# Turning 28 leftover dK^T/dV^T slabs in the input-gradient stage instead of the wq/wo-gradient stage

## The chip, the cores and the metric

One Trainium2 chip; the kernel runs on 1 of its cores. The metric is device time in microseconds of one execution of the whole program. Beside the timed runs there is one profiled execution, from which all rows of the profile come.

## The reference

The reference is a forward pass and its whole backward pass (a VJP). The forward normalizes `x`, runs attention over a K/V cache and a gated feed-forward layer on the same normalized input, and multiplies the two:

```python
def _fwd_reference(A_x, A_k_cache, A_v_cache, A_wq, A_wo, B_x, B_w_gate, B_w_up, B_w_down):
    def _A_ref(x, k_cache, v_cache, wq, wo):
        q = (x @ wq).reshape(B, Sq, H, Dh).transpose(0, 2, 1, 3)
        scores = jnp.einsum("bhqd,bhkd->bhqk", q, k_cache) * (Dh ** -0.5)
        p = _softmax(scores, axis=-1)
        o = jnp.einsum("bhqk,bhkd->bhqd", p, v_cache)
        return o.transpose(0, 2, 1, 3).reshape(B, Sq, H * Dh) @ wo
    def _B_ref(x, w_gate, w_up, w_down):
        h = _sigmoid(x @ w_gate) * (x @ w_up)
        return h @ w_down
    xn = _layernorm(A_x, axis=-1)
    s = _A_ref(xn, A_k_cache, A_v_cache, A_wq, A_wo)
    g = _silu(_B_ref(xn, B_w_gate, B_w_up, B_w_down))
    return A_x + s * g
```

The outputs are the forward result and the gradients of `x`, `k_cache`, `v_cache`, `wq`, `wo`, `w_gate`, `w_up` and `w_down` for a given `grad_out`. Sizes: S = 2048 positions, D = 576, H = 32 heads of Dh = 128, F = 4608; all tensors bfloat16. The gradients of the two caches have 32 x 2048 x 128 elements each, 0.52 MB a head.

## The kernel before

The kernel runs in stages, one after the other, each with its own tile pools.

1. Normalization and the first half of the feed-forward layer.
2. Its second half.
3. Attention, forward and backward, head by head. It produces dK and dV of each head **transposed**, as a slab of 128 x 2048, and puts the 64 slabs into a scratch tensor in DRAM, `kvT_d[h, k]` (k = 1 for dV, 0 for dK).
4. The output of the attention block, and the forward result.
5. The feed-forward weight gradients: a loop over 18 blocks `fb` of 256 columns of F.
6. The gradients of `wq` and `wo`: 8 groups `hg` of 4 heads. For each head two accumulations (`accumulate`, L982) of 16 row tiles with 2 matmuls each (512 and 64 columns): one gives the rows of dwo, the other the transposed dwq. ACT copies the result out of PSUM (L40). The dwo rows are stored from POOL's queue (L1143, two `dwo` buffers); dwq is turned by a transposing DMA on SP's queue (L1145) and stored per group (L990, L992). At the start of a group POOL issues the loads of the next group's attention output and dq, `onb` and `dqb` (L1010, L1013), 2 MB each. On SP, ten transposed weight pieces for the next stage (`load_T_rows`, L63) are spread over the first 20 heads. PSUM has room for four accumulations.
7. The input gradient: 8 blocks of 256 rows (`sbi`, class `Rows`), each the sum of three products with the transposed weights: du (36 row tiles of F), dg (36) and dq (32). The work is cut into 80 chunks, `seq`: 3 chunks of 12 tiles for du, 3 for dg, 4 chunks of 8 tiles for dq per block. The first two blocks run interleaved by product, so that block 0 ends at chunk 15 and block 1 at chunk 19; the others end at 29, 39 and so on to 79. A chunk is loaded by one transposing DMA on SP (`load_chunk`, L1122) into one of four buffers (two in the old `ah` tile, two called `cf`); chunk n therefore waits until TensorE is done with chunk n - 4. The matmuls are those of L1188. When a block is complete, ACT and DVE work on its two row tiles (`finish`, L1204 to L1217), and POOL stores them (`dx`, L1218); `got` loads (L1177) are issued on POOL where a block begins.

The slabs are turned to the natural layout by the pair `kv_turn` and `kv_store`: `kv_turn` takes the next slab, lets SP issue a transposing DMA from `kvT_d` into one of two `kvn` buffers (L1022), and `kv_store` lets POOL store that buffer into the output (L1028). Stage 5 calls the pair twice per block, which is 36 slabs. The 28 that are left are turned one per head in stage 6: `kv_turn` at the start of a head, `kv_store` at its end.

Two things set the order. Stages 4 to 7 run under a manual schedule for SP and POOL: each of these two queues issues its DMAs in the order in which the program text calls them, and a DMA that waits (for its data, or for a buffer) holds everything behind it on its queue. The other engines also work in program order. And a pool of a later stage takes the space of an earlier one, tile by tile as this comes free.

Of the kernel before, what the change touches and what calls it, by code (L numbers as in the profile page):

```python
# [66 lines left out]
def kernel(  # L67
# [8 lines left out]
    _, S, D = A_x.shape  # L76
    _, H, Sk, Dh = A_k_cache.shape
# [490 lines left out]
    for dead, flat in enumerate([t_[:].rearrange("p a b -> p (a b)") for t_ in (dsT, Kns[H % 2], Vn, dOn)] + [xnT_flat]):  # L568
        h0 = sum(n for _, _, n, _ in wo_parts)
        n = min(flat.shape[1] // D, H - h0)  # L570
# [314 lines left out]
    with late("pc") as pc, late("pcw") as pcw, late("pcf") as pcf, \  # L885
# [129 lines left out]
        kv_left = [(h, k) for h in range(H) for k in (1, 0)]  # L1015
        kv_wait = []

        def kv_turn(pool):
            if kv_left:
                h, k = kv_left.pop(0)  # L1020
                t_ = pool.tile([P, NT, P], bf, name="kvn", bufs=2)
                nc.sync.dma_start_transpose(t_[:], kvT_d[h, k])  # L1022
                kv_wait.append((t_, (out_2, out_3)[k][0, h]))

        def kv_store():
            if kv_wait:
                t_, dst = kv_wait.pop(0)
                nc.gpsimd.dma_start(dst.rearrange("(p t) d -> p t d", t=NT), t_[:])  # L1028
# [75 lines left out]
        seq = []  # L1104
# [14 lines left out]
        def load_chunk(n):  # L1119
            sbi, (src_d, nK, KC), k0 = seq[n]  # L1120
            v = bufs4[n % len(bufs4)][:, :KC * SB2].rearrange("p (k s) -> p k s", s=SB2)
            nc.sync.dma_start_transpose(v, src_d[sbi * SB2:(sbi + 1) * SB2, k0 * P:(k0 + KC) * P])  # L1122
            return v

        chunks = {}
        with late("c2w") as wp, late("c2b") as blk, late("c2s", 2) as sb, late("c2ps", 4, space=PSUM) as ps:
            dqTs = padded(wp, 2, "dqT")
            onqs = [(onb0, dqb0), tuple(blk.tile([P, NT, HG * P], bf, name=nm)[:] for nm in ("onb", "dqb"))]
            gap = max(1, (H - HG) // len(wT_pieces))
            for hg in range(NHG):  # L1130
                cols = slice(hg * HG * P, (hg + 1) * HG * P)
                onb, dqb = onqs[hg % 2]
                if hg + 1 < NHG:
                    load_on(onqs[(hg + 1) % 2][0], hg + 1)
                    load_dq(onqs[(hg + 1) % 2][1], hg + 1)
                dwq = dwqs[hg % 2]
                for hl in range(HG):
                    h = hg * HG + hl
                    lcols = slice(hl * P, (hl + 1) * P)
                    kv_turn(blk)  # L1140
                    dwo = sb.tile([P, D], bf, name="dwo")
                    accumulate(ps, onb, ds_all, lcols, dwo, "acc")
                    nc.gpsimd.dma_start(out_5[h * P:(h + 1) * P, :], dwo[:])  # L1143
                    accumulate(ps, dqb, xn_all, lcols, dqTs[h % 2], "acc")
                    nc.sync.dma_start_transpose(dwq[:, :, lcols], dqTs[h % 2][:])  # L1145
                    kv_store()
                    if h % gap == gap - 1 and wT_pieces:
                        load_T_rows(nc, *wT_pieces.pop(0))
                    if hg == NHG - 1 and hl < len(cf_pre) and NHG % 2 == 0:
                        chunks[hl] = load_chunk(hl)  # L1150
                store_T(out_4, cols, dwq)
            while wT_pieces:
                load_T_rows(nc, *wT_pieces.pop(0))
            while kv_left or kv_wait:
                kv_turn(blk)
                kv_store()

        with late("c4s", 2) as sb, late("c4cf") as chp, late("c4ps", 2, space=PSUM) as ps:
            wqT_sb = wd_flat[:, :H * D].rearrange("p (h d) -> p h d", d=D)
            assert H * D <= DT * F  # L1160
            wq_pieces = list(dts)
            total_k = FT * 2 + H
            cf_more = [chp.tile([P, cf_n], bf, name=f"cf{k}")[:] for k in range(2)]
            npre = len(chunks)
            order4 = list(range(len(cf_pre)))
            bufs4[:] = cf_pre + cf_more
            ahead = [npre]

            class Rows:

                def __init__(self, sbi):
                    self.sbi = sbi
                    self.accs = [[ps.tile([P, 512], f32, name=f"acc{sl}_{j}") for j in range(len(ncs))] for sl in range(nsl)]
                    self.gots = []
                    for sl in range(nsl):
                        got = sb.tile([P, D], bf, name=f"got{sl}")
                        nc.gpsimd.dma_start(got[:], go2[(sbi * nsl + sl) * P:(sbi * nsl + sl + 1) * P, :])  # L1177
                        self.gots.append(got)
                    self.k = 0

                def mul(self, ch, wT, k0, KC):
                    last = self.k + KC == total_k
                    order = [(kk, sl) for kk in range(KC) for sl in range(nsl)]
                    if last:
                        order.sort(key=lambda o: o[1])
                    for kk, sl in order:
                        for j, (n0, nn) in enumerate(ncs):
                            nc.tensor.matmul(self.accs[sl][j][:, :nn], lhsT=ch[:, kk, sl * P:(sl + 1) * P], rhs=wT[:, k0 + kk, n0:n0 + nn],  # L1188
                                             start=(self.k + kk == 0), stop=(self.k + kk == total_k - 1))
                    self.k += KC  # L1190
                    if last:
                        self.finish()

                def finish(self):
                    nj = len(ncs)
                    for sl in range(nsl):
                        st = self.sbi * nsl + sl
                        rows = slice(st * P, (st + 1) * P)
                        dxn = sb.tile([P, D], f32, name="dxn")
                        ca = sb.tile([P, nj], f32, name="ca")  # L1200
                        cb = sb.tile([P, nj], f32, name="cb")
                        junk = sb.tile([P, D], f32, name="junk")
                        for j, (n0, nn) in enumerate(ncs):
                            nc.scalar.activation(dxn[:, n0:n0 + nn], self.accs[sl][j][:, :nn], AF.Copy, accum_out=ca[:, j:j + 1])  # L1204
                            nc.vector.scalar_tensor_tensor(junk[:, n0:n0 + nn], self.accs[sl][j][:, :nn], 1.0, xn_all[:, st, n0:n0 + nn],  # L1205
                                                           op0=ALU.mult, op1=ALU.mult, accum_out=cb[:, j:j + 1])
                        cs = sb.tile([P, 2], f32, name="cs")
                        nc.vector.tensor_reduce(cs[:, 1:2], cb[:], axis=AX.X, op=ALU.add)
                        nc.vector.tensor_reduce(cs[:, 0:1], ca[:], axis=AX.X, op=ALU.add)
                        m12 = sb.tile([P, 2], f32, name="m12")  # L1210
                        nc.vector.tensor_scalar(m12[:], cs[:], -1.0 / D, None, op0=ALU.mult)
                        t = sb.tile([P, D], f32, name="t")
                        nc.vector.scalar_tensor_tensor(t[:], xn_all[:, st, :], m12[:, 1:2], dxn[:], op0=ALU.mult, op1=ALU.add)
                        t2 = sb.tile([P, D], f32, name="t2")
                        nc.vector.tensor_scalar(t2[:], t[:], m12[:, 0:1], rstd_all[:, st:st + 1], op0=ALU.add, op1=ALU.mult)
                        dx = sb.tile([P, D], bf, name="dx")
                        nc.vector.tensor_tensor(dx[:], t2[:], self.gots[sl][:], op=ALU.add)  # L1217
                        nc.gpsimd.dma_start(o1[rows, :], dx[:])  # L1218

            row_of = {}  # L1220
            for n, (sbi, which, k0) in enumerate(seq):
                if n not in chunks:
                    chunks[n] = load_chunk(n)
                if n % 2 and n >= 3 and wq_pieces:
                    load_T_rows(nc, wqT_sb, A_wq, *wq_pieces.pop(0))
                if sbi not in row_of:
                    row_of[sbi] = Rows(sbi)
                wT = wuT_sb if which is fu else wgT_sb if which is fg else wqT_sb
                if which is fq:
                    while wq_pieces:  # L1230
                        load_T_rows(nc, wqT_sb, A_wq, *wq_pieces.pop(0))
                row_of[sbi].mul(chunks.pop(n), wT, k0, which[2])
        pc3.release()


# [28 lines left out]
```

## Time and profile before

| what | value |
| --- | --- |
| five runs, us | 5067.85, 5022.1, 5056.59, 5067.54, 5031.59 |
| median of these, us | 5056.59 |
| the profiled execution, us | 5059.62 |
| its span, us | 5057.8 |
| mean granted TensorE clock | 0.988 |
| busy: TensorE, VectorE, ScalarE, GpSimd | 4896.9, 2530.7, 2501.3, 887.8 us |
| stage 6, first to last matmul, us from the span's start | 4302.2 to 4629.8 |
| stage 7, first to last matmul | 4629.8 to 5045.9 |

In the profile's rows PE is TensorE, DVE VectorE, ACT ScalarE, POOL GpSimd, SP the sync engine. A row of a group gives line, engine, output and inputs; a row of a wait reads "who, its line, <- the engine and line waited for: total us, times, longest us". A DMA is counted from its issue to its landing. The DMA share is the mean busy time of the core's 16 DMA engines; where transfers overlap in an engine it can pass 1.

### The profile page before, as it was taken

How to read it: one execution, taken by the hardware profiler on the slowest of the kernel's cores; microseconds unless marked ns; L12 is line 12 of the kernel's file. 1: busy time of each engine (PE TensorE's matmuls, PEld its weight loads, DVE VectorE, ACT ScalarE, POOL GpSimd, SP SyncE). 2: the span in 40 equal slices, each digit the busy share in tenths (PEclk: the TensorE clock that was granted, in tenths of full speed). 3: DMA queues.
4: the chain of work that ended last, by engine and by line, in shares of the span. 5: the costliest groups of instructions: out<-in, count | busy, mean ns of one | idle time of the engine just before them, and what ended most of it. 6: DMA issues, size and time to landing. Idle time of an engine off the chain costs nothing.

```text
span 5057.8 us, 102037 instructions
## 1 busy us (share of the span) xinstructions
PE 4896.9 (97%) x41029; PEld 2901.3 (57%) x41029; DVE 2530.7 (50%) x6625; ACT 2501.3 (49%) x4576; POOL 887.8 (18%) x1379
## 2 busy tenths in 40 slices
PE   9999999999999999999999999998999999878999
PEld 4445666666666666666666666665565555434554
DVE  4544665665665665665665665665254443000111
ACT  4422766666666666666666666665132222111000
POOL 3322111111111111111111111111222322111000
PEclk9999999999999999999999999999999999999999
DMA  7887999999999999999999999999899999999976
GB/s 259 273 205 171 229 231 216 231 228 226 230 231 224 225 225 228 231 223 223 235 231 222 227 235 222 227 225 230 208 223 256 235 230 261 272 256 241 172 140 120
DMA packets 3053831, 1134.86 MB, mean 224 GB/s; under 512 B 2948321, under 2 KB 2952546, under 8 KB 3053346
## 3 DMA queue, kind: packets, MB, share of 16 engines
q1 hardware_dynamic: 2944738, 771.06, 83.2%
q0 software_dynamic: 108000, 356.60, 22.6%
q8 instruction: 322, 5.28, 0.4%
q14 instruction: 163, 1.34, 0.1%
q10 hardware_dynamic: 608, 0.59, 0.0%
HBM read 175.31 MB, written 215.68 MB: 77 GB/s over the span
## 4 chain that ended last, share of the span: by engine, by line
PE 85%; DMA 8%; SPq 3%; issue 2%; DVE 2%; POOL 1%; ACT 0%; POOLq 0%; ACTq 0%; DVEq 0%
PE acc L685 18%; PE acc L746 16%; PE sp L638 9%; PE dp L708 8%; PE acc L982 8%; PE acc L1188 7%; PE acc L217 5%; PE u_ps L452 3%; PE g_ps L450 3%; PE acc L535 2%; PE dh L1059 2%; PE acc L952 2%; DMA ah<-h_d 2%; SPq L1022 1%; PE acct L147 1%
## 5 line engine op out<-in xcount | busy, mean ns | idle before, releaser
L656 ACT ACTIVATE Pq<-sp 128x1024 bf16<-128x1024 f32 x1024 | 1047.0, 1023 | 274.2 <-PE sp L638 264.9
L711 DVE SCALAR_TENSOR_TENSOR Pq<-dp,negdelta,Pq 128x1024 bf16<-128x1024 f32 x512 | 654.8, 1279 | 44.8 <-PE dp L708 44.7
L714 ACT ACTIVATE t<-dp,negdelta 128x1024 bf16<-128x1024 f32 x512 | 567.1, 1114 | 215.1 <-PE dp L708 200.5
L708 PE MATMUL dp<-VT,dOT 128*128 128x512 bf16 x2048 | 609.7, 379 | 2.2
L638 PE MATMUL sp<-KQ 128*128 128x512 bf16 x2048 | 609.5, 379 | 2.2 <-ACT Pq L656 2.1
L685 PEld LDWEIGHTS <-dST 128*128 128x128 bf16 x8192 | 508.4, 98 | 157.2 <-DMA dST<-Pq 17.2
L685 PEld LDWEIGHTS <-PT 128*128 128x128 bf16 x8192 | 500.4, 98 | 139.2 <-DMA PT<-Pq 20.2
L685 PE MATMUL acc<-Kn,dST 128*128 128x128 bf16 x8192 | 557.7, 219 | 11.4 <-DMA dST<-Pq 11.4
L685 PE MATMUL acc<-Vn,PT 128*128 128x128 bf16 x8192 | 543.0, 219 | 13.5 <-DMA PT<-Pq 13.0
L746 PE MATMUL acc<-Pq,dOn 128*128 128x512 bf16 x2048 | 531.9, 379 | 0.0
L746 PE MATMUL acc<-Pq,Qn 128*128 128x512 bf16 x2048 | 526.5, 380 | 0.0
L715 DVE TENSOR_TENSOR Pq<-t,Pq 128x1024 bf16<-128x1024 bf16 x512 | 354.4, 692 | 322.5 <-ACT t L714 308.1
L1205 DVE SCALAR_TENSOR_TENSOR junk<-acc,xn_all 128x512 f32<-128x512 f32 (+1 forms) x32 | 13.9, 453 | 718.8 <-ACT dxn L1204 718.8
L726 ACT ACTIVATE dq_n<-acc,rsc 128x128 bf16<-128x128 f32 x512 | 187.5, 366 | 339.3 <-PE acc L685 317.8
L746 PEld LDWEIGHTS <-Qn 128*128 128x128 bf16 x2048 | 200.5, 98 | 241.3 <-issue 2.4
L746 PEld LDWEIGHTS <-dOn 128*128 128x128 bf16 x2048 | 199.0, 98 | 234.5 <-issue 1.1
L638 PEld LDWEIGHTS <-KQ 128*128 128x128 bf16 x2048 | 179.2, 98 | 124.1 <-issue 3.6
L708 PEld LDWEIGHTS <-dOT 128*128 128x128 bf16 x2048 | 178.7, 98 | 124.0 <-issue 11.7
L679 POOL DMA_DIRECT2D on_d<-o_n x128 | 97.1, 759 | 782.7 <-DVE junk L697 462.2
L643 DVE TENSOR_REDUCE rs_all<-rsp 128x1 f32<-128x2 f32 x512 | 78.4, 153 | 306.3 <-ACT Pq L656 295.5
L679 POOL DMA_DIRECT2D dq_d<-dq_n x128 | 98.0, 765 | 713.0 <-ACT dq_n L726 671.4
L1060 DVE SCALAR_TENSOR_TENSOR nbl<-ah 128x256 bf16<-128x256 bf16 x288 | 98.7, 417 | 236.8 <-DMA ah<-h_d 227.6
(210 smaller groups left out, 6734.8 us busy)
## 6 DMA issues: line engine op xcount, KB each, us to landing
out_dram<-kvn POOLq DMA_DIRECT2D x64, 512.0 KB, 8.8
ah<-a_d POOLq DMA_DIRECT2D x18, 1024.0 KB, 9.6
ah<-h_d POOLq DMA_DIRECT2D x18, 1024.0 KB, 12.4
du_d<-du_blk POOLq DMA_DIRECT2D x18, 1024.0 KB, 14.5
dg_d<-dg_blk POOLq DMA_DIRECT2D x18, 1024.0 KB, 16.3
h_d<-h_row POOLq DMA_DIRECT2D x64, 256.0 KB, 3.5
a_d<-a_row POOLq DMA_DIRECT2D x64, 256.0 KB, 3.8
x_all<-in_A_k_cache_dram SPq DMA_DIRECT2D x64, 256.0 KB, 3.7
```

The source lines that it names most:

```text
L217: nc.tensor.matmul(av[:, :CH], lhsT=w[:, i, :], rhs=srcT[:, i, cs], start=(i == 0), stop=(i == DT - 1))
L638: nc.tensor.matmul(sp[:, c * CH:(c + 1) * CH], lhsT=hs.QT[:, qt * P:(qt + 1) * P], rhs=hs.KT[:, hf * HW_ + c * CH: hf * HW_ + (c + 1) * CH ...
L656: nc.scalar.activation(Pq[:, hsl], sp[:], AF.Exp, scale=SCALE, accum_out=hs.rsp[:, hf:hf + 1])
L679: nc.gpsimd.dma_start(dst_d[q0 * P:(qt + 1) * P, hs.h * P:(hs.h + 1) * P].rearrange("(t p) d -> p t d", p=P), buf[:])
L685: nc.tensor.matmul(hs.acc[:, 0, :], lhsT=T[:, kt, :], rhs=rhs[:, kt, :], start=(kt == 0), stop=(kt == NT - 1))
L708: nc.tensor.matmul(dp[:, c * CH:(c + 1) * CH], lhsT=hs.dOT[:, qt * P:(qt + 1) * P], rhs=hs.VT[:, hf * HW_ + c * CH: hf * HW_ + (c + 1) * C ...
L711: nc.vector.scalar_tensor_tensor(Pq[:, hsl], dp[:], hs.negdelta[:, qt:qt + 1], Pq[:, hsl], op0=ALU.add, op1=ALU.mult)
L714: nc.scalar.activation(t[:], dp[:], AF.Identity, bias=hs.negdelta[:, qt:qt + 1], scale=1.0)
L715: nc.vector.tensor_tensor(Pq[:, hsl], t[:], Pq[:, hsl], op=ALU.mult)
L746: nc.tensor.matmul(self.acc, lhsT=self.nat[:, qt, :], rhs=self.slabs[qt][:, cs], start=(qt == self.lo), stop=(qt == self.hi - 1))
L982: nc.tensor.matmul(accs[j][:, :nn], lhsT=lhs[:, st, cols], rhs=rhs[:, st, n0:n0 + nn], start=(st == 0), stop=(st == NT - 1))
L1188: nc.tensor.matmul(self.accs[sl][j][:, :nn], lhsT=ch[:, kk, sl * P:(sl + 1) * P], rhs=wT[:, k0 + kk, n0:n0 + nn], start=(self.k + kk == 0) ...
```

## The change

The calls of `kv_turn` and `kv_store` in the loop over heads of stage 6 are taken out, and the loop that emptied the list at its end. Stage 7 calls them instead: from chunk 10 on, at every even chunk, after the chunk's load and before its matmuls, `kv_store` of the slab before and then `kv_turn` of the next one, as many as the pace formula gives. After the last slab is turned, `kv_store` follows the matmuls of the chunk. The two `kvn` buffers now come from the pool `c4cf` of stage 7.

```diff
@@ stage 6, the loop over the heads of a group
                     lcols = slice(hl * P, (hl + 1) * P)
-                    kv_turn(blk)
                     dwo = sb.tile([P, D], bf, name="dwo")
                     accumulate(ps, onb, ds_all, lcols, dwo, "acc")
                     nc.gpsimd.dma_start(out_5[h * P:(h + 1) * P, :], dwo[:])
                     accumulate(ps, dqb, xn_all, lcols, dqTs[h % 2], "acc")
                     nc.sync.dma_start_transpose(dwq[:, :, lcols], dqTs[h % 2][:])
-                    kv_store()
...
             while wT_pieces:
                 load_T_rows(nc, *wT_pieces.pop(0))
-            while kv_left or kv_wait:
-                kv_turn(blk)
-                kv_store()
@@ stage 7, the loop over the chunks
                 if n not in chunks:
                     chunks[n] = load_chunk(n)
+                if n >= len(seq) // 8 and n % 2 == 0:
+                    for _ in range(-(-len(kv_left) // max(1, (len(seq) * 7 // 8 - n) // 2))):
+                        kv_store()
+                        kv_turn(chp)
                 if n % 2 and n >= 3 and wq_pieces:
                     load_T_rows(nc, wqT_sb, A_wq, *wq_pieces.pop(0))
...
                 row_of[sbi].mul(chunks.pop(n), wT, k0, which[2])
+                if not kv_left:
+                    kv_store()
+            while kv_left or kv_wait:
+                kv_turn(chp)
+                kv_store()
```

## The prediction

> **What bounds the kernel now.** I read four things in this order: the slices of the page, the busy times of the two last stages, the waits inside the first of them, and the queues inside the second. All durations come from the one profiled execution (5059.6 us in all, span 5057.8). It lies 3 us above the median of the five runs, 5056.6; those reach from 5022 to 5068, so that about 1% is what a measurement of this kernel can tell from no change.
>
> The slices first; 40 of 126 us each.
>
> ```profile
> PE   9999999999999999999999999998999999878999
> ```
>
> TensorE is the bound nearly everywhere. The one dip at the end is slices 34 to 36, and the stages there are the wq/wo gradients (PE from 4302.2 to 4629.8 us) and the start of the input gradient (4629.8 to the end). The next view is busy time by stretch: PE, weight loads, DVE, ACT, POOL, granted clock, DMA share, GB/s.
>
> ```profile
> 4302.00:4598.00 296.00, 231.45 (x1792) 117.14 (x1793) 0.00 (x0) 36.07 (x105) 54.59 (x83) 0.90 1.09 271
> 4598.00:4630.00 32.00, 31.60 (x259) 16.38 (x259) 0.00 (x0) 7.21 (x23) 6.15 (x11) 1.00 0.98 217
> 4660.00:4700.00 40.00, 40.00 (x328) 20.56 (x327) 0.00 (x0) 0.00 (x0) 0.00 (x0) 1.00 1.10 226
> 4760.00:5000.00 240.00, 240.00 (x1961) 124.34 (x1960) 32.17 (x100) 8.92 (x40) 9.18 (x17) 1.00 0.77 145
> ```
>
> In heads 0 to 27 of wq/wo, the heads with a slab turn, PE is busy 231 of 296 us while the DMA engines are full (1.09). In heads 28 to 31, which have none, PE is full. The input gradient keeps PE full; its DMA share is 1.10 at the start and 0.77 later. Now the waits inside wq/wo.
>
> ```profile
> POOL out_dram L1028 <- DMA kvn<-kvT_d: 246.7, 27, 18.7
> ACT dwo L40 <- DMA out_dram<-dwo: 222.6, 27, 23.9
> PE acc L982 <- ACT dwo L40: 62.2, 7, 17.5
> ```
>
> Read from the bottom: PE waits for a free accumulator, which ACT has not copied out, because the dwo buffer's store (L1143) has not landed. That store sits on POOL behind a kvn store (L1028), and POOL stands still until the slab's turn has landed. All the long PE waits stand at the start of a group of four heads, where 4 MB of the next on/dq blocks is loaded as well.
>
> **The change part by part.** 36 of the 64 slabs are turned under the feed-forward gradients, before and after. The other 28 leave the heads: 28 transposes on SP (L1022) and 28 stores on POOL (L1028), each of 0.52 MB. They reappear in the input gradient, one pair at every even chunk n from 10 to 64 of 80 (the pace formula gives 1 each time), and the last store is issued well ahead of the end, so that the last row's tail (last matmul 5045.9, span 5057.8) stays.
>
> *Taken out of wq/wo.* 64 accumulations of 3.92 us start to start (32 matmuls) are 250.9 us. The stage took 4629.8 - 4302.2 = 327.5. What is left, 76.6, is 64.8 of waits at accumulator copies (62.2 and 2.6), some 9 us of five slow restarts (5.79 instead of 4.08 us for 32 matmuls after a wait of 17.5, and the like after each of 7.7 or more; none after 3.0), one more such restart at the stage's start (1.8), and crumbs. With the slab turns gone the DMA engines carry 87.1 - 29.4 = 57.7 MB here; at the 266 GB/s of this stage 217 us, under 251. So DMA is no longer the bound, and nothing stands ahead of a dwo store but its group's loads. These still hold it for some 17 us, against two heads (15.7 us) until its buffer is wanted and two more of accumulator buffers. Best: 252.7 us, a gain of 75 (only the first restart remains). Worst: each of six group starts keeps the shortest of the long waits, 7.7 us, a gain of 29. I take 70, near the best, because heads 28 to 31 (31.5 us) and the first eight heads ran without a wait.
>
> ```profile
> 4598.40 31.52 PE acc L982 x256
> ```
>
> This is the last group in the chain that ended last: 256 matmuls, 123 ns each.
>
> *Added to the input gradient, by throughput.* Chunks 10 to 64 are 31 of 5.88 us (du/dg, 0.786 MB) and 24 of 3.92 us (dq, 0.524 MB): 276.4 us of PE. Their transposes are 37.0 MB, one late wq piece 1.05, the 28 slabs 14.7: 52.7 MB. At the 226 GB/s of the stretch 4660 to 4700, which moved almost nothing but transposes at a full share, 233 us. Plain transfers are 14.7 MB of slab stores and 3.5 of got and dx. The rate of these I work out from wq/wo, where both kinds ran at a full share:
>
> ```profile
> q1 hardware_dynamic: 128978, 32.42, 60.4%
> q0 software_dynamic: 14691, 54.38, 47.3%
> ```
>
> 32.4 MB of transposes at 226 GB/s leave 184.5 of the 328 us for 54.4 MB: 295 GB/s. So 18.2 MB are 62 us, and the sum 295 against 276: 18 us too much. If the two kinds overlap better than here, nothing; if the DMA engines also stand idle at the six row finishes described below, up to 60: SP is held for 6.4 + 5.0 us there, and the stores and got loads of that time (1.1 MB at 295 GB/s) fill 4, which leaves some 7 idle each time.
>
> The Trainium skill's page Advanced Engine Details and Errata, section X-Bar Transpose (TRN2), says that transposing transfers are as fast as plain ones and to expect 350 to 400 GB/s. The row of 226 GB/s at a share of 1.10 doesn't agree, and the measurement decides; by the page the 52.7 MB would be an estimated 151 us, this term would vanish, and the sum would be 18 us lower.
>
> *Added to the input gradient, by order.* This is the wait that takes the place of the old one. A chunk load (L1122) waits until PE is done with the chunk four before it. A slab turn waits on SP for the store of the slab two before it (two kvn buffers), and this store stands on POOL in program order, behind the dx stores (L1218) of a row that finishes at chunk f. Rows finish at f = 15, 19, 29, 39, 49 and 59 in the range of the slabs. Then the store at f+1 can't be issued before the row is finished, the turn at f+3 waits for it, and load f+4, queued behind this turn, is late; PE waits for that load. The pieces of one finish as it is now (PE, POOL and SP of the timeline):
>
> ```profile
> 4783.06 8.00 PE L1188 MATMUL acc<-wdT_sb,ah 128*128 128x512 bf16 x64
> 4791.10 2.92 SPq L1122 DMA_TRANSPOSE ah<-dg_d  x1
> 4796.95 0.55 POOL L1218 DMA_DIRECT2D out_dram<-dx  x1 [2.25 <-DVE dx L1217]
> ```
>
> PE ends chunk 29 at 4791.06; load 33 starts 0.04 us later; the second dx store is done on POOL at 6.4. After the change load 33 comes behind: 6.4, the slab store's landing 5.0 (median in wq/wo), the turn on SP 3.5 (median), and lands 5.2 later: 20.1 after the finish. PE has three chunks until then: 17.6 us where they are du/dg (five finishes, 2.5 late each), 11.8 where they are dq (f = 15, 8.3 late, and a slow restart of 1.8). Sum 22.6, taken as 23. With the shortest rows (2.9, 1.6, 4.4) it is 15.3: 3.5 late once and nothing else. With long ones (8.8, the page's median of all slab stores; 3.6; 10.3, the longest chunk landing) it is 29.1: 11.5 five times and 17.3, and six slow restarts, 86 in all.
>
> *At nothing.* POOL's 28 issues of 0.54 us and SP's issues between chunk loads (per two du/dg chunks 2 x 3.1 + 3.5 of 11.8 us): SP has the room except around n = 10, where it is one or two chunks ahead only, and that is in the throughput term. The kvn tiles' new place: the third and fourth chunk buffers wait for the last group's operands anyway (PE 6.0 us late at 4653.6); a place that frees earlier or later moves that by at most these 6 us either way.
>
> **Sum.** -70 + 18 + 23 = -29: 5059.6 - 29 = 5030.6, and 5028 from the median. I say 5030.
>
> **The rivals.** (a) *The turns hide nearly whole.* The later rows' share of 0.77 speaks for it, and that a late load is absorbed by the three loaded chunks; against it that slabs and chunks together ask for more than the transposes' rate shown. -70 + 4 + 6 for an uneven start: 5000. (b) *The order on POOL costs more than it saves; slower than before.* Place: load f+4 at six finishes. Price by the long rows 86, with the throughput term 18 and half of the lost gaps (21) 125: 5059.6 - 70 + 125 = 5115. It decides from (70 - 18)/6 = 8.7 us lost per finish; a saturated queue, where a slab took up to 31 us to land, speaks for it, and that only the slab store and one turn are in flight at that moment speaks against. (c) *The waits in wq/wo aren't the slabs' doing.* All long waits stand at group starts, with the on/dq loads; if these hold the dwo stores alone, the gain is 29, and with 41 given back the time is 5072. Against it speak the first two groups, which load as much and have no wait.
>
> **How the numbers follow.** Forecast 0.50, its own range 5008 to 5050; (a) 0.23; (b) 0.13; (c) 0.14. Below 5006 lie (a) and a little of the forecast: 0.25. Above 5107 lies rather more than half of (b): 0.09. The rest is within 1%: 0.66. The range takes in the best of (a), 4988, and leaves out most of (b) only: 4988 to 5085.
>
> **What would show it.** In the profile after: wq/wo stage of 253 to 262 us with POOL's wait at L1028 and ACT's wait at dwo nearly gone, PE full in it; the input gradient some 41 us longer; waits of PE at L1188 for cf or ah tiles right after chunks 18, 22, 32, 42, 52 and 62, of 2 to 10 us, with SP waiting at L1022 for the kvn store and POOL at L1218 ahead of it; DMA share near 1.1 from 4615 to 4900 us. If PE still waits at group starts in wq/wo, the first term is wrong; if the waits at L1188 lie anywhere else or the stage grows by more than 70 us, the second.

## The result and the profile after

The changed kernel takes 5018.0 us in the median, the kernel before 5056.6: a ratio of 0.9926, 95% interval [0.9907, 0.9945], which is 28 to 47 us less. The profiled execution has a span of 5002.9 us, 54.9 below the one before. In what follows a stage's length runs from its first matmul to the next stage's first one, the last stage's to the end of its last matmul.

| | before | after | difference |
| --- | --- | --- | --- |
| stages 1 to 5, start to first matmul of stage 6 | 4302.2 | 4293.4 | -8.8 |
| stage 6 (wq/wo) | 327.5 | 252.6 | -74.9 |
| stage 7 (input gradient) | 416.1 | 443.8 | +27.7 |
| last matmul to the end of the span | 11.9 | 13.1 | +1.2 |

The first row isn't the edit's: over the executions shown below the start of stage 6 lies between 4279 and 4337 us, whatever is changed behind it. That scatter is nearly as wide as the spread of the runs before, and is why stage lengths are used here beside the times. Where no second execution is named, a stage length is that of one profiled execution.

The start of stage 7 scatters too, with no slab in it yet. These rows of PE show the wait in its first six chunks before the change and the row with which chunk 6 begins (L1188 before the change is L1183 after it):

```profile
4653.57 8.13 PE L1188 MATMUL acc<-wuT_sb,cf 128*128 128x512 bf16 x48 [6.02 <-DMA cf<-du_d]
4673.30 11.93 PE L1188 MATMUL acc<-wgT_sb,cf 128*128 128x512 bf16 x96
```

and after:

```profile
4583.41 11.94 PE L1183 MATMUL acc<-wgT_sb,cf 128*128 128x512 bf16 x96 [0.83 <-DMA cf<-dg_d]
```

So the first six chunks took 43.6 us before and 37.5 after. The first slab is turned only behind the load of chunk 10, and the same changed kernel took 42.9 us for them in a second execution; over all executions shown here it is 35.3 to 44.9, with slabs in the stage or without. From chunk 6 to the end the stage took 372.6 us before and 406.4 after (406.8 in the second execution). The slabs' price in stage 7 is therefore better read as 33.8 us than as 27.7: the profiled execution happened to save 6.1 at the start.

The slices of the page: the dip has moved out of slices 34 to 36, and small ones have come at the end.

```profile
PE   9999999999999999999999999999899999999898
```

Busy time by stretch (PE, weight loads, DVE, ACT, POOL, clock, DMA share, GB/s), for stage 6, for the part of stage 7 with the slabs, and for what follows it:

```profile
4293.40:4546.00 252.60, 252.60 (x2049) 130.33 (x2050) 0.00 (x0) 43.44 (x126) 45.97 (x66) 0.99 0.82 228
4610.00:4915.00 305.00, 278.49 (x2218) 140.85 (x2216) 39.22 (x120) 10.72 (x48) 26.94 (x50) 0.98 1.14 227
4915.00:4990.00 75.00, 74.76 (x612) 38.30 (x608) 7.88 (x28) 2.86 (x13) 2.16 (x4) 1.00 0.71 132
```

Stage 6 has no idle PE any more, and its DMA share has fallen from 1.09 to 0.82. Stage 7 has a full DMA share while slabs are turned, and PE idles there for 26 of 305 us. The waits of stage 6, that had 222.6 us at this line:

```profile
ACT dwo L40 <- DMA out_dram<-dwo: 42.3, 5, 8.9
```

Now PE in stage 7, six of its rows that begin with a wait (the bracket gives the idle time before the row and what ended it). They are the ones at the places that the prediction named; ten more waits, of 0.5 to 2.4 us, lie elsewhere behind the start of chunk 6:

```profile
4662.40 6.06 PE L1183 MATMUL acc<-wdT_sb,cf 128*128 128x512 bf16 x32 [6.22 <-DMA cf<-dq_d]
4686.96 6.05 PE L1183 MATMUL acc<-wgT_sb,cf 128*128 128x512 bf16 x48 [0.86 <-DMA cf<-dg_d]
4741.41 6.05 PE L1183 MATMUL acc<-wgT_sb,ah 128*128 128x512 bf16 x48 [1.31 <-DMA ah<-dg_d]
4796.59 6.05 PE L1183 MATMUL acc<-wgT_sb,cf 128*128 128x512 bf16 x48 [1.25 <-DMA cf<-dg_d]
4852.15 6.05 PE L1183 MATMUL acc<-wgT_sb,ah 128*128 128x512 bf16 x48 [1.67 <-DMA ah<-dg_d]
4905.31 6.05 PE L1183 MATMUL acc<-wgT_sb,cf 128*128 128x512 bf16 x48 [0.84 <-DMA cf<-dg_d]
```

These are chunks 19, 23, 33, 43, 53 and 63, the ones the prediction named. The first also shows the slow restart (6.06 us for 32 matmuls; 4.09 where the wait was short). How the first comes about, from the rows of PE, POOL and SP:

```profile
4644.25 2.80 SPq L1122 DMA_TRANSPOSE cf<-dq_d  x1
4650.59 0.55 POOL L1213 DMA_DIRECT2D out_dram<-dx  x1 [2.32 <-DVE dx L1212]
4651.13 1.07 POOL L1028 DMA_DIRECT2D out_dram<-kvn  x2
4654.08 3.19 SPq L1022 DMA_TRANSPOSE kvn<-kvT_d  x1
4657.35 1.92 SPq L1122 DMA_TRANSPOSE cf<-dq_d  x1
```

SP stands from 4647.05 (4644.25 + 2.80) to 4654.08, since the slab's buffer is freed by a store that POOL issues only behind the dx store; the chunk load behind it starts at 4657.35, and PE waits for it until 4662.40.

### The profile page after: what moved, and what is told of

The parts are those of the page before. It is cut to its first block, busy times and chain, and to the rows that moved or that the text cites. A ratio compares the mean times of both kernels' runs of the same rounds, so it can differ in the third digit from the quotient of the medians.

```text
span 5002.9 us, 102058 instructions
## 1 busy us (share of the span) xinstructions
PE 4892.3 (98%) x41029; PEld 2897.0 (58%) x41029; DVE 2531.1 (51%) x6625; ACT 2503.9 (50%) x4576; POOL 891.1 (18%) x1379
## 4 chain that ended last, share of the span: by engine, by line
PE 87%; DMA 6%; issue 3%; DVE 2%; SPq 2%; ACT 0%; POOL 0%; POOLq 0%; ACTq 0%; DVEq 0%
PE acc L685 18%; PE acc L746 17%; PE acc L982 11%; PE sp L638 9%; PE dp L708 9%; PE acc L217 5%; PE acc L1183 5%; PE u_ps L452 3%; PE g_ps L450 3%; PE acc L535 3%; PE dh L1059 2%; PE acc L952 2%; DMA ah<-h_d 2%; PE acct L147 1%; DVE Pq L711 1%
## 5 line engine op out<-in xcount | busy, mean ns | idle before, releaser
L1199 ACT ACTIVATE dxn<-acc 128x512 f32<-128x512 f32 (+1 forms) x32 | 12.8, 407 | 429.6 <-PE acc L1183 422.0
```

## The experiments

**Without the 28 slabs.** Edit, ahead of stage 6:

```diff
+        kv_left.clear()
         chunks = {}
```

> The changed kernel without the 28 slabs of stage 7: they are neither turned nor stored, so these parts of the two cache gradients are left out. Theory: stage 7 is longer after the change only because of the slabs, by 24 us (439.8 against 416.1 from its first to its last matmul), and stage 6 is free of them already. Then stage 7 takes 414 to 420 us here, stage 6 stays at 253 to 258, and the time is some 24 us below the changed kernel's, about 60 us below the kernel before (ratio near 0.988). Rival: part of the 24 us comes from something else that moved with the edit (the earlier start of stage 7, other buffer places); then stage 7 stays above 425.

(The 439.8 us in this expectation start some 4 us too late; by the definition above it is 443.8, an excess of 27.7.) Measured: stage 6 252.4 us, stage 7 416.1, as in the kernel before, and 372.8 from chunk 6 on (372.6 before); ratio to before 0.984 [0.9774, 0.9905]. So the whole excess of stage 7 is the slabs', and stage 6 gains nothing more from their absence than the changed kernel has already.

**Stage 6 with its stores on the other queue.** The kernel before, with `kv_store` taking the queue as an argument (POOL where none is given) and

```diff
+                    kv_store(nc.sync)
                     kv_turn(blk)
...
-                    kv_store()
```

> The kernel before, with the slab stores of stage 6 issued on SP at the start of the next head (ahead of the next turn) instead of on POOL at the end of the head. The same bytes move. Order theory for the old stalls: POOL stood at the slab store until the turn had landed, and the dwo stores behind it came late; with POOL free the PE waits at dwo nearly vanish and stage 6 takes 255 to 275 us in place of 327.5. Throughput theory: 87 MB at some 266 GB/s are the limit, stage 6 stays above 310 us, whichever queue issues the stores. Between: both play a part.

Measured: stage 6 330.1 us, time ratio 0.9985 [0.996, 1.0009]. PE's wait for the dwo copies is as long as before:

```profile
PE acc L982 <- ACT dwo L40: 63.3, 6, 14.1
```

The order theory of the old stalls, as put on record, falls. POOL's standing at the slab store was what the profile named; it is gone, and with the same bytes at 261 GB/s, the DMA engines full (share 1.03), the dwo stores come late all the same. But the run moves the waiting rather than takes it away. SP now stands at the slab stores, the dwq transposes behind them come late, and POOL and ACT wait for these (0.7 and 28.8 us in the kernel before):

```profile
POOL out_dram L990 <- DMA wdT_sb<-dqT: 109.7, 6, 23.2
ACT dqT L40 <- DMA wdT_sb<-dqT: 92.0, 20, 8.3
```

So this run alone doesn't exclude that an order, now on SP's queue, holds the stage. The next one has no slab store on any queue.

**Stage 6 with the turns alone.** The kernel before, stage 6 with `kv_wait.clear()` in place of `kv_store()`:

> The kernel before with the 28 slabs turned in stage 6 but not stored (these parts of the cache gradients are left out). POOL has no slab store to wait at. 87.1 - 14.7 = 72.4 MB are left. Throughput theory by bytes at 266 GB/s: 272 us against 250.9 of PE work, stage 6 takes 268 to 280. Theory of slow turns (a turn beside the group loads moves little and holds SP): the turns are still there, stage 6 stays above 295. Order theory, which the stores on SP spoke against: 253 to 258.

Measured: 281.3 us, with the DMA engines full (share 1.03, 257 GB/s). The bytes' estimate was 272 and its range ended at 280; the measured time lies 1.3 above it and well off the other two ranges, so the bytes' theory holds, somewhat short. From 252.6 us without slabs, the turns alone cost 28.7, and the stores beside them the other 46.2 of the 74.9. (The stores without the turns were not tried.)

**Four kvn buffers in stage 7**, to take the wait of SP away (`kv_turn` takes their number as an argument):

```diff
-                        kv_turn(chp)
+                        kv_turn(chp, 4)
...
-                        junk = sb.tile([P, D], f32, name="junk")
+                        junk = sb.tile([P, D], f32, name="junk", bufs=1)
```

(likewise for t and t2).

> The changed kernel with four kvn buffers in stage 7 in place of two (room for them comes from single buffers for junk, t and t2, which only DVE touches). Order theory: the waits at chunks 19, 23, 33, 43, 53 and 63, 12 us and a slow restart of 2 in the changed kernel, come from a turn that waits for a store behind the dx stores; with two more buffers the turn need not wait, SP's waits at L1022 for the kvn store (29.2 us) go to nearly 0, and stage 7 takes 424 to 430 us. Throughput theory: the DMA engines are the limit, the waits only move to other chunks, and stage 7 stays at 436 to 444.

Measured: neither. This wait of SP in the changed kernel's stage 7

```profile
SPq L1022 <- DMA out_dram<-kvn: 29.2, 6, 6.9
```

is gone, and the stage takes 474.9 us, 31 more than with two buffers (432.2 from chunk 6 on, 26 more). The time ratio to before is 0.9935 [0.9906, 0.9965]. Two controls. The single buffers alone:

> The changed kernel with two kvn buffers and only the other edit of the four-buffer run: single junk, t and t2 buffers. If the four kvn buffers made that run's stage 7 slow (474.9 against 443.8 us), stage 7 is 440 to 448 here. If the single buffers, or the places in SBUF that follow from them, did it, it is above 465.

Measured 453.3 us, which lies between the two ranges; 414.1 from chunk 6 on, against 406.4 and 406.8 in the changed kernel. So the single buffers cost some 8 us of the 26, by one execution. And the four buffers again:

> The kernel with four kvn buffers in stage 7 once more, for its stage length alone. If the store traffic that no longer waits in turn with the transposes makes stage 7 slow, it is 465 to 485 us again, against 443.8 and 449.7 in the changed kernel and 453.3 with the single buffers alone. If 474.9 was one execution's, it is 440 to 455.

Measured 482.2 us (438.3 from chunk 6 on), so it repeats: beyond the single buffers the four cost 18 and 24 us. (That they also lie at other places in SBUF is a rival that no run tests.) What happens without the wait is seen by comparing the two traces behind the end of the same row block (chunk 29). Busy time by stretch of the four-buffer kernel:

```profile
4742.00:4748.00 6.00, 6.00 (x52) 3.05 (x50) 0.27 (x1) 0.00 (x0) 2.69 (x5) 1.00 1.33 272
4748.00:4754.00 6.00, 6.00 (x51) 3.17 (x50) 0.00 (x0) 0.00 (x0) 0.00 (x0) 1.00 1.07 98
4754.00:4760.00 6.00, 0.32 (x4) 0.01 (x1) 0.00 (x0) 0.00 (x0) 0.00 (x0) 0.90 1.18 116
```

and of the changed kernel:

```profile
4728.00:4734.00 6.00, 6.00 (x51) 3.05 (x49) 0.06 (x1) 0.00 (x0) 2.68 (x5) 1.00 1.10 342
4734.00:4740.00 6.00, 6.00 (x50) 3.02 (x48) 0.00 (x0) 0.00 (x0) 0.55 (x1) 1.00 0.94 216
```

In both POOL issues a burst here: a dx store, two slab stores, two got loads. In the changed kernel SP issues nothing from 4728.6 to 4733.9, and the burst is through at 342 GB/s. In the four-buffer kernel SP goes on, with a slab turn at 4743.49 and a chunk load at 4749.94; the DMA engines are as full, but move about 100 GB/s for 12 us, and PE runs dry. The DMA queues (packets, MB, share) of those 12 us, 4748 to 4760:

```profile
q1 hardware_dynamic: 2350, 0.59, 83.6%
q0 software_dynamic: 204, 0.69, 28.9%
```

The transposes' queue holds the engines for 84% and moves 0.59 MB. The second execution has the same, most plainly behind chunk 49: the burst, a turn and a chunk load, then 81 and 91 GB/s at shares of 1.20 and 1.22 in two stretches of 6 us, and a wait of PE of 12.3 us. Why transposes and stores are so slow there no run here shows.

**The turns alone in stage 7** (`kv_wait.clear()` in place of the stores):

> The changed kernel with the 28 slabs turned in stage 7 as before but not stored: these parts of the two cache gradients are left out. No turn waits for a store then, and 14.7 MB of plain traffic are gone. If the turns alone fill the DMA engines beside the chunk loads (transposes 52.7 MB at 226 GB/s, 233 us of 276), stage 7 keeps more than half of its 27.7 us: above 430 us. If the loss comes from the stores, by their bytes beside the transposes and by their place in the order, it falls to 416 to 424.

Measured: stage 7 421.6 us, 378.5 from chunk 6 on. 28 turns alone cost some 6 us; the stores, by their bytes and by their place in the order together, the other 28 of the 33.8.

**The stores of stage 7 on SP**, in one line with the transposes (all but the last, which stays on POOL):

```diff
-                        kv_store()
+                        kv_store(nc.sync)
                         kv_turn(chp)
```

> The changed kernel with the slab stores of stage 7 issued on SP just ahead of the next turn instead of on POOL. Order theory: the store no longer stands behind the dx stores of a finished row, the waits of 2 to 6 us at chunks 19, 23, 33 and so on go, and stage 7 takes 424 to 430 us; SP then waits for the last turn's landing before each store, which it has time for. Throughput theory: stage 7 stays at 436 to 444 us. A loss (above 445) would show that SP, which issues the chunk loads too, has no room for the wait.

Measured: stage 7 434.3 us, ratio 0.9872 [0.9828, 0.9916]. Once more, beside the changed kernel:

> The kernel with all 28 stores of stage 7 on SP once more, beside the changed kernel on the same chip: stage 7 at 430 to 438 us by the order theory (434.3 the first time), and 5 to 12 us faster than the changed kernel.

> The changed kernel once more, to see how far one execution's stage lengths can be trusted: stage 6 at 252 to 254 us, stage 7 at 438 to 450 if its waits repeat. If it goes past 460, the 474.9 us of the four-buffer kernel says nothing on its buffers.

Measured: 437.0 against 449.7 us of stage 7; ratios to before 0.9888 [0.9841, 0.9936] and 0.9898 [0.9859, 0.9937]. By the stage lengths, two executions of each, the queue is worth 7 to 15 us, and 8 to 11 from chunk 6 on (398.0 and 395.5 against 406.4 and 406.8); the times don't tell the two apart. The first execution's 434.3 lies between the ranges of both theories, so the order is some part of the excess; what the rest is, this run doesn't say. The bytes and the turns are the same, and only the way in which stores and transposes follow each other differs.

**Eight slabs back in stage 6**, where the changed kernel leaves room (heads 22 to 29), 20 in stage 7 with stores on SP:

```diff
+                    if 22 <= h < 30:
+                        kv_turn(blk)
```

(and `kv_store()` at the end of the same heads).

> Meant to beat both: stores of stage 7 on SP as in the last run of the first set, and 8 of the 28 slabs turned back in stage 6, in heads 22 to 29, where the changed kernel's DMA share is 0.5 to 0.7; 20 are left for stage 7. By bytes: 8 slabs add 8.4 MB to some 62 us at 150 GB/s, 285 GB/s at most, so stage 6 grows by 0 to 8 us from 252.6; stage 7 gives back 8/28 of its 18.2 us excess in that run, 5 us, to 429. Sum 682 to 690 us for both stages against 696.4 in the changed kernel and 743.6 before; ratio to the kernel before 0.985 to 0.99. If slow turns beside the group loads hold here too, stage 6 is above 265.

Measured: stage 6 252.7 us, so the eight are free; stage 7 436.5, no better for having eight fewer (396.6 from chunk 6 on); ratio 0.9869 [0.982, 0.9918]. Its 20 slabs still come at every second chunk, from 10 to 48, and half of its excess of 24 us lies before chunk 20. So, with the pace and the first chunk, 18, as the only further edits:

```diff
-                if n >= len(seq) // 8 and n % 2 == 0:
-                    for _ in range(-(-len(kv_left) // max(1, (len(seq) * 7 // 8 - n) // 2))):
-                        kv_store(nc.sync)
-                        kv_turn(chp)
+                if n >= 18 and n % 3 == 0:
+                    kv_store(nc.sync)
+                    kv_turn(chp)
```

> As the split of 8 and 20 slabs, but stage 7 takes its 20 slabs at every third chunk from 18 to 75 in place of every second from 10 to 48: past the crowded start with the wq pieces and the dq chunks of the first two blocks, and at 194 GB/s (du/dg) and 222 GB/s (dq) of transposes and slab stores in place of 225 and 270. If the DMA engines' load by stretch is what is left of stage 7's excess, it falls from 436.5 to 418 to 425 us, stage 6 stays at 253, and the time is 8 to 15 us below the kernel with the stores on SP. If the place makes no difference, it stays at 432 to 438.

Measured: stage 6 253.0 us, stage 7 417.6, from chunk 6 on 372.8, as without slabs; ratio to before 0.980 [0.9752, 0.9848]. This beats both kernels; the changed one ran at 0.9898 [0.9859, 0.9937] beside it. All waits of PE in its stage 7 are these:

```profile
PE acc L1187 <- DMA cf<-du_d: 6.3, 1, 6.3
PE acc L1187 <- DMA cf<-dg_d: 1.1, 1, 1.1
```

The first is the one at the stage's start that the kernel before has too (6.0); the second is at chunk 6, before any slab. Whether the sparser pace or the later start does it, no run separates.

| kernel | stage 6 | stage 7 | both | stage 7 from chunk 6 on |
| --- | --- | --- | --- | --- |
| before | 327.5 | 416.1 | 743.6 | 372.6 |
| changed, two executions | 252.6, 252.6 | 443.8, 449.7 | 696.4, 702.3 | 406.4, 406.8 |
| no slabs (left out) | 252.4 | 416.1 | 668.5 | 372.8 |
| turns alone in stage 7 (stores left out) | 253.8 | 421.6 | 675.4 | 378.5 |
| four kvn buffers, two executions | 252.4, 253.4 | 474.9, 482.2 | 727.3, 735.6 | 432.2, 438.3 |
| single buffers alone | 253.0 | 453.3 | 706.3 | 414.1 |
| stage 7 stores on SP, two executions | 252.6, 250.9 | 434.3, 437.0 | 686.9, 687.9 | 398.0, 395.5 |
| 8 + 20, every second chunk | 252.7 | 436.5 | 689.2 | 396.6 |
| 8 + 20, every third chunk | 253.0 | 417.6 | 670.6 | 372.8 |

## Why the prediction was right, and which terms were not

The forecast was 5030 us by a large gain in stage 6, of which stage 7 gives some back. The median is 12 us lower, in the forecast's own range; the misses in the two stages, 5 and 7 us, go the same way.

*Taken out of wq/wo*: -70 predicted, -74.9 measured, the best case of 75. The reason given was right where it went by bytes: 57.7 MB fit under 251 us of PE work. The sentence that a dwo store stands behind a kvn store on POOL described the profile, but with the slab stores on SP the stage is as long (330.1 us), and with turns alone it is still 281.3 with full DMA engines; so what sets the time is the bytes rather than that place in the order. Rival (c), that the group loads alone hold the dwo stores, is refuted by the changed kernel itself, which has these loads and in which PE doesn't wait at all.

*Added by throughput and by order*: 18 + 23 = 41 predicted, 33.8 measured from chunk 6 on, 34.3 in the second execution. The stage's 27.7 has the shorter start in it (6.1 us), which the prediction had put at nothing, with up to 6 us either way; the second execution (33.6) hasn't, so the lower figure was luck. The size that was off is the order term: the waits at the six named chunks add up to 12.2 us (6.22, 0.86, 1.31, 1.25, 1.67, 0.84) and one slow restart to 2.0: 14, where 23 stood. Load 19 began 3.3 us after the turn that held it up, near the 3.5 assumed, but after the du/dg finishes chunks came on average 1.2 us late and not 2.5. The other 19 or 20 us lie at other chunks, where 18 stood for throughput. By the prediction's own sign, waits elsewhere speak against its second term. That they come to about 18 doesn't show the term right either, since no run separates throughput from order: the turns alone cost 6 us, the stores the other 28, and moving the stores to SP's queue, with the same bytes, took 8 to 11 off.

That the two terms could be added as if independent is the step that the runs don't bear out. The order's wait was priced as a loss, of 3.5 to 86 us; taking it away cost 18 and 24 us more beyond the single buffers. That it had kept POOL's stores and SP's turns apart is how the two traces read; no run tests it by itself. The throughput term's rate was also somewhat high: its figures make 70.9 MB in 295 us, 240 GB/s, and the stretch from 4610 to 4915 ran at 227 with a full share.

Rival (a), nearly whole hiding, is what the kernel with every third chunk reaches (372.8 us from chunk 6 on, 372.6 in the kernel before); the changed kernel's pace doesn't. Rival (b) stayed far from its price: 125 us of loss, 34 measured.

The Trainium skill's page DMA: Bandwidth & Descriptors, section Issuing engines are not separate DMA queues, says that transfers issued by SP, ACT and POOL run on the same 16 engines and interleave, and that issuing them from several engines at once saves only issue time. Stage 6 agrees (327.5 and 330.1 us with the stores on either queue); in stage 7 the issuing queue made 8 to 11 us all the same.

The 350 to 400 GB/s for transposes of the page cited in the prediction weren't seen in the stretch of transposes alone (4660 to 4700 before the change): it ran at 226, and its fastest microsecond at 291.

## What to carry to other kernels

A wait that the profile names for most of the idle time may be only the place where a full resource is felt: before you price it, move the wait with the bytes unchanged, and look where the waiting goes. When work is moved into a stage with free DMA share, ask how it lies against that stage's demand chunk by chunk: here 28 slabs at every second chunk cost 34 us, and 20 at every third from chunk 18 on, with 8 in the heads that had room and the stores on SP, cost nothing that can be seen. A stage's length can hide scatter at its start: compare it from the first point that the change touches. And taking away a wait that orders two kinds of traffic can cost more than the idle time it shows.

## What the runs showed of the hardware

A full DMA share is no measure of what is moved. In the worst 12 us the engines were counted busy (shares 1.07 and 1.18) at 98 and 116 GB/s, with 0.59 MB of transposes and 0.69 MB of plain transfers. In the changed kernel the same burst ran at 342 GB/s at a share of 1.10, with SP issuing nothing and 0.56 MB of transposes, of a chunk load issued before, beside it. So it isn't enough that both kinds are there. What the slow stretch has besides is a slab turn in flight with the slab stores: it took 16.9 us from issue to landing, and the one that the changed kernel issued behind its burst 4.5. That this is what makes it slow is not shown. Stage 7 with four buffers had a full share over its whole length (1.07 at 195 GB/s; the changed kernel 1.06 at 209), and was the longest of all.
